# Two decode layers on one core: attention by groups of four heads from one row of DRAM, with more kept on chip for the second layer

## The chip, the cores and the metric

The kernel runs on one core of a Trainium2 chip. The metric is device time in microseconds, taken over three runs of the kernel. The profile is one execution recorded by the hardware profiler.

## What is computed

Four sequences (B = 4), one token each, 640 features, float32. Attention and a gated MLP are applied twice, in turn, with the same weights and the same caches:

```python
x = A_x
x = x + _A_ref(_layernorm(x), A_k_cache, A_v_cache, A_wq, A_wo)
x = x + _B_ref(_layernorm(x), B_W_gate, B_W_up, B_W_down)
x = x + _A_ref(_layernorm(x), A_k_cache, A_v_cache, A_wq, A_wo)
x = x + _B_ref(_layernorm(x), B_W_gate, B_W_up, B_W_down)

# _A_ref: 32 heads of 128, the last W = 1024 of 4096 cached keys
q = (x @ wq).reshape(B, 1, 32, 128).transpose(0, 2, 1, 3)
p = softmax(einsum("bhqd,bhkd->bhqk", q, k) * 128 ** -0.5)
o = einsum("bhqk,bhkd->bhqd", p, v)
return o.transpose(0, 2, 1, 3).reshape(B, 1, 4096) @ wo

# _B_ref: F = 1728
gate, up = x @ W_gate, x @ W_up
return (gate * (gate > 0) * up) @ W_down
```

Per layer the four caches and matrices are 329,024 floats for each of the 128 partitions. All the arithmetic is one row per sequence, so each weight and each cached key is used once or four times and then not needed until the second layer.

## The kernel before

Everything that is read more than once lies in one SBUF tile, `store`, of 54,560 floats per partition. `heads` in DRAM holds for each of the 32 heads one block of 128 rows of 9,472 floats: 640 of the query weights (WQ), 4,096 of keys (KK), 4,096 of values (VV), 640 of the output weights (WO). `mlp` holds the MLP's 25,920 floats per partition: the gate and up weights in four parts (the last part, narrower, first), then the down weights.

**Loads.** `todo` (lines 67 to 107) is the list of loads in order, written out by hand. `load` (115) issues the next one on SP's DMA queue into the ring `store` as soon as its whole place is free; `done` (144) marks a place free after the last product that reads it and calls `load` again. SP issues in order, so a load that waits for its place holds all later ones back. The program order of the products thus sets which product each load waits for. Loads of the first 27 heads are whole heads. Heads 27 (its second half) to 31 stay on chip for layer two: in layer one they go to the front of `store`, up to FRONT = 42,624, and `done` does not free them. The first MLP uses what lies behind FRONT, 11,936 floats. Layer two takes the heads in the order 27 to 31, 0 to 26 (line 66).

**Attention** (313) works head by head, one ahead: the query of the next head (230: five products of 128 columns, with the normalized x repeated eight times to fill 32 rows), its scaling on VectorE (240) and turn (244), then for a head the scores (250: eight products of 512 columns, one for each sequence and half of the keys, four of them side by side in the four column strips of TensorE), softmax on VectorE and ScalarE (262), the turn of the probabilities (269: eight transposes), the values (278: eight products of 512 columns), the sums (290), the turn of the four sequences' outputs (296) and the projection into `y` (305). `y` stays in PSUM and gathers the residual.

**The MLP** (352) works in four parts: gate and up products (358), ReLU and product (369), a turn (378), the down products (391).

Between the stages `normalized` (182) and `deviation` (212) do the layer norm from `y`; `go_on` (224) puts the residual back into `y`. The last two lines of the kernel copy `y` and store it.

Of the kernel before, what the change touches and what calls it, by code (L numbers as in the profile page):

```python
# [21 lines left out]
WQ, KK, VV, WO = 0, D, D + 4096, D + 8192  # L22
HALF = D + 4096
HEAD = 2 * HALF

# [8 lines left out]

STORE = 54560
KEPT = 5

FRONT = KEPT * HEAD - HALF  # L40
FIRST, FIRST_MLP = 10928, 51880


CUTS = {
    "head": [*range(WQ, KK, P), *range(KK, WO, 512), *range(WO, HEAD + 1, QUARTER)],
    "mlp": [*range(0, GU0, P), *range(GU0, WD0, 256), WD0, TAIL, *range(WD1, MLP + 1, D)],
}
# [3 lines left out]
def decode_kernel(ctx: ExitStack, tc: tile.TileContext, x, heads, mlp, sel, out):  # L51
# [4 lines left out]
    ps_s = ctx.enter_context(tc.tile_pool(name="ps_s", bufs=1, space=bass.MemoryType.PSUM))  # L56
    ps_p = ctx.enter_context(tc.tile_pool(name="ps_p", bufs=2, space=bass.MemoryType.PSUM))
    ps_o = ctx.enter_context(tc.tile_pool(name="ps_o", bufs=1, space=bass.MemoryType.PSUM))
    ps_y = ctx.enter_context(tc.tile_pool(name="ps_y", bufs=1, space=bass.MemoryType.PSUM))
    ps_m = ctx.enter_context(tc.tile_pool(name="ps_m", bufs=2, space=bass.MemoryType.PSUM))  # L60
# [5 lines left out]
    order = [list(range(H)), list(range(H - KEPT, H)) + list(range(H - KEPT))]  # L66
    todo = []

    def pieces(layer, kind, i, *cuts):
        for lo, hi in zip(cuts, cuts[1:]):  # L70
            todo.append((layer, kind, i, lo, hi))

    def half_a(layer, h, step=4096):
        pieces(layer, "head", h, WQ, *range(KK + step, VV, step), VV)

    def half_b(layer, h, step=4096):
        pieces(layer, "head", h, VV, *range(VV + step, WO, step), HEAD)

    for h in range(H - KEPT):
        pieces(0, "head", h, 0, HEAD)  # L80
    split = H - KEPT
    half_b(0, split)
    half_a(0, split)
    half_a(0, split + 1)
    for h in range(split + 1, H - 1):
        half_a(0, h + 1)
        pieces(0, "head", h, VV, WO)

    pieces(0, "head", H - 1, VV, VV + 3072, WO)
    for h in range(split + 1, H):  # L90
        pieces(0, "head", h, WO, HEAD)
    pieces(0, "mlp", 0, 0, *[c for j in range(3) for c in (GU0 + j * GU, GU0 + j * GU + 2048)],
           WD0, WD1 + WD, WD1 + 2 * WD, MLP - 2 * D, MLP - D, MLP)
    half_b(1, split, 2048)
    steps = [2048] * 6 + [4096] * 2
    half_a(1, 0, steps[0])
    for h in range(7):
        half_a(1, h + 1, steps[h + 1])
        half_b(1, h, steps[h])
    half_b(1, 7)  # L100
    for h in range(8, split):
        pieces(1, "head", h, 0, HEAD)
    pieces(1, "mlp", 0, 0, *range(GU0 + GU, WD0 + 1, GU), *range(WD1 + WD, MLP - WD + 1, WD),
           MLP - 2 * D, MLP - D, MLP)

    jumps = {(0, "head", split, 0): 0, (0, "mlp", 0, 0): FIRST_MLP, (1, "head", split, VV): FRONT}
# [3 lines left out]
    at = FIRST  # L110
    source = {"head": heads, "mlp": mlp}

    held = {}

    def load(part=False):

        nonlocal at
        while todo:
            layer, kind, i, lo, end = todo[-1]
            at = jumps.pop((layer, kind, i, lo), at)  # L120
            hi = max(c for c in CUTS[kind] + [end] if c <= min(end, lo + STORE - at))
            if hi <= lo:
                at = FRONT if layer == 0 and kind != "head" else 0
                continue
            if any(live[at:at + hi - lo]):
                n = live.index(True, at) - at
                hi = max([lo] + [c for c in CUTS[kind] if c <= lo + n])
                if not part or hi < lo + 512:
                    return
            todo.pop()  # L130
            if hi < end:
                todo.append((layer, kind, i, hi, end))
            live[at:at + hi - lo] = [True] * (hi - lo)
            held.setdefault((layer, kind, i), []).append((lo, hi - lo, at))
            nc.sync.dma_start(out=store[:, at:at + hi - lo], in_=source[kind][i][:, lo:hi])
            at += hi - lo

    def get(key, lo, n):
        for first, m, p in held[key]:
            if first <= lo and lo + n <= first + m:  # L140
                return store[:, p + lo - first:p + lo - first + n]
        raise KeyError((key, lo, n))

    def done(key, lo, n):

        if key[1] == "head" and key[0] == 0 and (key[2] > split or key[2] == split and lo < VV):
            return
        for first, m, p in held[key]:
# [9 lines left out]
    sel_sb = const.tile([P, P + 40], F32, name="sel_sb")  # L158
# [3 lines left out]
    nc.vector.memset(eps_sb, EPS)  # L162

# [323 lines left out]
```

## Time and profile before

| | |
|---|---|
| three runs | 755.49, 757.39 (median), 758.18 us |
| profiled execution, span from first to last instruction | 754.4 us |
| runs' median less that span | 2.95 us |
| read from DRAM | 315.19 MB |
| loads issued on SP's queue | 101 of heads, 22 of the MLP |
| busy TensorE / weight loads / VectorE / ScalarE | 604.2 / 301.0 / 174.8 / 121.3 us |
| mean granted TensorE clock | 0.832 |

The page gives the profiled execution's span alone; its own time as a run is not among its lines. TensorE's busy time counts overlapping and pipelined products, and the granted clock is a share of full speed. A load's time to landing is counted from its issue, so it includes the time in the queue behind earlier loads.

### The profile page before, as it was taken

What the parts mean: (1) busy time and instruction counts of PE and PEld (TensorE: products, weight loads), DVE (VectorE), ACT (ScalarE), POOL (GpSimd) and SP (SyncE); (2) the same over time, 40 slices, a digit from 0 to 9 for tenths busy, and PEclk for the clock granted to TensorE, in tenths of its full rate; (3) what the DMA queues carried; (4) which work ended last, traced back from release to release, by engine and by line L of the source; (5) the groups of instructions that cost most, each with busy time, mean ns of one, the idle gap of its engine ahead of it and who ended that gap; (6) DMA issues with size and microseconds to landing.
All of it is one profiled execution on the core that took longest, in us unless ns stands there. A gap on an engine that the chain in (4) does not pass through costs nothing.

```text
span 754.4 us, 11650 instructions
## 1 busy us (share of the span) xinstructions
PE 604.2 (80%) x5150; PEld 301.0 (40%) x5150; DVE 174.8 (23%) x495; ACT 121.3 (16%) x218; POOL 0.2 (0%) x4
## 2 busy tenths in 40 slices
PE   0788678787788697888867888888887787797888
PEld 0344343344344243344433444444443343343344
DVE  0222212212212221222211222323221222221221
ACT  1201111111101101112201111111211111111120
POOL 0000000000000000000000000000000000000000
PEclk9988788778878877789997888989988788877878
DMA  9999999999999999999999999999999999999994
GB/s 389 433 423 435 440 421 443 419 437 430 426 437 424 434 427 434 423 427 423 408 378 420 401 414 415 432 434 433 422 428 444 421 441 423 437 423 429 431 423 175
DMA packets 18058, 316.02 MB, mean 419 GB/s; under 512 B 2004, under 2 KB 2644, under 8 KB 4696
## 3 DMA queue, kind: packets, MB, share of 16 engines
q1 hardware_dynamic: 17856, 315.19, 98.2%
q8 instruction: 40, 0.66, 0.3%
q10 hardware_dynamic: 152, 0.10, 0.0%
q14 instruction: 10, 0.08, 0.0%
HBM read 315.19 MB, written 0.08 MB: 418 GB/s over the span
## 4 chain that ended last, share of the span: by engine, by line
DMA 60%; PE 28%; DVE 5%; ACT 4%; issue 3%; SPq 0%; ACTq 0%; DVEq 0%
DMA store<-in_heads 57%; PE ps L257 9%; PE so L300 5%; DVE nm L265 4%; PE pp L275 4%; DMA store<-in_mlp 3%; PE y L309 2%; ACT probs L267 2%; PE gu L365 2%; ACT gates L288 1%; PE so L292 1%; PE qt L246 1%; PE qp L236 1%; PE po L285 1%; PE y L396 1%
## 5 line engine op out<-in xcount | busy, mean ns | idle before, releaser
L257 PE MATMUL ps<-store,qT 128*32 128x512 f32 x1024 | 190.8, 884 | 2.3 <-ACT probs L267 1.3
L267 ACT ACTIVATE probs<-ps,nm 128x1024 f32<-128x1024 f32 x64 | 71.3, 1113 | 558.1 <-DVE nm L265 558.1
L285 PE MATMUL po<-store,pT 128*32 128x512 f32 x1024 | 124.7, 605 | 0.0
L236 PE MATMUL qp<-store,xT 128*32 128x128 f32 x640 | 45.4, 308 | 82.5 <-DMA store<-in_heads 81.4
L300 PE MATMUL so<-sel_sb,gates 128*128 128x1 f32 x512 | 78.9, 275 | 28.2 <-ACT gates L288 28.2
L300 PEld LDWEIGHTS so<-sel_sb,gates 128*128 128x128 f32 x512 | 73.7, 222 | 45.1 <-ACT gates L288 37.9
L236 PEld LDWEIGHTS qp<-store,xT 128*32 128x32 f32 x640 | 28.3, 118 | 133.0 <-DMA store<-in_heads 115.8
L265 DVE TENSOR_REDUCE nm<-ps 128x1 f32<-128x1024 f32 x64 | 77.8, 1215 | 7.5 <-PE ps L257 7.5
L275 PE MATMUL pp<-sel_sb,probs 128*128 128x128 f32 x512 | 77.4, 300 | 0.0
L275 PEld LDWEIGHTS pp<-sel_sb,probs 128*128 128x128 f32 x512 | 72.0, 174 | 0.0
L257 PEld LDWEIGHTS ps<-store,qT 128*32 128x32 f32 x1024 | 38.4, 140 | 75.6 <-issue 63.6
L294 DVE RECIPROCAL r<-so 128x4 f32<-128x4 f32 x64 | 11.7, 183 | 224.6 <-PE so L292 224.6
L292 PEld LDWEIGHTS so<-sel_sb,sm 128*128 128x128 f32 x128 | 24.9, 243 | 89.8 <-issue 84.3
L242 DVE TENSOR_SCALAR qs<-qp,rstd 128x128 f32<-128x128 f32 x64 | 22.4, 351 | 146.1 <-PE qp L236 145.9
L285 PEld LDWEIGHTS po<-store,pT 128*32 128x32 f32 x1024 | 26.9, 109 | 50.2 <-DVE pT L276 29.4
L276 DVE COPY pT<-pp 128x128 f32<-128x128 f32 x128 | 37.3, 292 | 38.1 <-PE pp L275 29.9
L288 ACT COPY gates<-po 128x512 f32<-128x512 f32 x64 | 36.8, 575 | 5.8 <-PE po L285 5.8
L309 PE MATMUL y<-store,oT 128*4 128x160 f32 x512 | 34.8, 354 | 1.6 <-DVE oT L303 0.5
L292 PE MATMUL so<-sel_sb,sm 128*128 128x4 f32 x128 | 30.5, 309 | 1.9 <-ACT probs L267 1.9
L303 DVE TENSOR_TENSOR oT<-so,r 128x4 f32<-128x4 f32 x64 | 10.4, 162 | 89.0 <-PE so L300 89.0
L246 PE MATMUL qt<-sel_sb,qs 128*128 128x4 f32 x128 | 27.5, 285 | 2.9 <-DVE qs L242 2.9
L246 PEld LDWEIGHTS qt<-sel_sb,qs 128*128 128x128 f32 x128 | 24.2, 236 | 4.2 <-DVE qs L242 2.8
(51 smaller groups left out, 123.7 us busy)
## 6 DMA issues: line engine op xcount, KB each, us to landing
store<-in_heads SPq DMA_DIRECT2D x38, 4736.0 KB, 41.7
store<-in_heads SPq DMA_DIRECT2D x10, 2368.0 KB, 40.4
store<-in_heads SPq DMA_DIRECT2D x13, 1344.0 KB, 11.5
store<-in_heads SPq DMA_DIRECT2D x13, 1024.0 KB, 9.7
store<-in_heads SPq DMA_DIRECT2D x2, 3648.0 KB, 37.9
store<-in_heads SPq DMA_DIRECT2D x2, 3392.0 KB, 41.2
store<-in_heads SPq DMA_DIRECT2D x3, 2048.0 KB, 40.2
store<-in_mlp SPq DMA_DIRECT2D x2, 2560.0 KB, 40.5
```

The source lines that it names most:

```text
L236: nc.tensor.matmul(qp[h][32 * g:32 * g + 32, :], xT[:, c], w, start=c < 4, stop=c > 0, tile_position=(0, 32 * g))
L246: nc.tensor.matmul(qt, qs.pop(h), sel_b, start=True, stop=True)
L257: nc.tensor.matmul(ps[32 * b:32 * b + 32, j, :], q[:, b:b + 1].to_broadcast([P, 32]), get(key, lo, 512), start=True, stop=True, tile_posit ...
L265: nc.vector.tensor_reduce(nm, flat, axis=AX.X, op=ALU.max, negate=True)
L267: nc.scalar.activation(probs, flat, AF.Exp, bias=nm, accum_out=sums[h])
L275: nc.tensor.transpose(pp[:, c, :], probs[:, (4 * j + c) * P:(4 * j + c + 1) * P], ident)
L276: nc.vector.tensor_copy(t[:, 4 * j:4 * j + 4], pp[:, :, None, 0:P:32].to_broadcast([P, 4, 8, B]))
L285: nc.tensor.matmul(po[32 * g:32 * g + 32, :], p[:, c], get(key, VV + c * 512, 512), start=c < 4, stop=c >= 4, tile_position=(0, 32 * g))
L288: nc.scalar.copy(gates, po)
L292: nc.tensor.matmul(so[h][:, :B], sums.pop(h).to_broadcast([P, P]), sel_s, start=True, stop=True)
L300: nc.tensor.matmul(s[:, B + b:B + b + 1], gates[:, b * P:(b + 1) * P], sel_b[:, b:b + 1], start=True, stop=True)
L309: nc.tensor.matmul(y[32 * g:32 * g + B], o, get(key, WO + g * QUARTER, QUARTER), start=False, stop=last, tile_position=(0, 32 * g))
```

## The change

Four heads make a group; there are eight groups. `heads` and `mlp` become one array, `stream`, of 128 rows of 329,024 floats: the pieces of all groups and of the MLP in the order in which they are used (q0, k0, q1, v0, o0, k1, q2, ...). A load is a run of columns of it, up to 13,700 floats.

A group is handled as one: its scores go into the same PSUM tile, row 32b + h for sequence b and head h. For that the turned query is written into a cleared tile `qz`, in which the four columns that serve head h are zero but for its own, and the four heads' products are added up in PSUM. One softmax, one turn and one sum then serve four heads. The values products of the four heads lie side by side in the four column strips. The query is one run of five products of 512 columns. A group's projection comes after the first scores of the next group.

Kept for layer two are group 7 (q7, k7, v7, o7), o6 and the last 7,680 floats of v6. They lie in front of KEPT = 48,128; `store` has 55,040 floats, so 6,912 remain behind them, three times SLOT = 2,304, and the first MLP goes through those. Layer two takes the groups in the order 7, 6, 0 to 5.

The shared PSUM tiles `ps`, `po`, `qp`, `ms` replace rotating ones; `go_on` moves behind the first scores, and in the MLP behind the first full gate part.

The core of the diff:

```diff
+GH = 4
+G = H // GH
+WQ, KV, WO = KC * GH * P, GH * 4096, GH * D
...
-STORE = 54560
-KEPT = 5
-FRONT = KEPT * HEAD - HALF
-FIRST, FIRST_MLP = 10928, 51880
+VKEPT = 7680
+SLOT = 2304
+FRONT = VKEPT + WO
+KEPT = FRONT + WQ + 2 * KV + WO
+STORE = KEPT + 3 * SLOT
+FIRST = 0
+LONG = 13700
...
+    steps(0, 0, WQ, 4096, 4096, 8192)
+    run(0, AT["k", 0] + KV, AT["q", 7])
+    run(0, AT["q", 7], AT["q", 7] + WQ, place=FRONT)
+    run(0, AT["v", 6], vsplit)
+    run(0, vsplit, AT["k", 7], place=0)
+    steps(0, AT["k", 7], *[4096] * 7, 2048, 1024, 1024, 1280, 1280, place=FRONT + WQ)
+    todo.append([KEPT])
+    run(0, M0, TOTAL - 3 * D, SLOT)
+    steps(0, TOTAL - 3 * D, 2 * D, D)
+    todo.append([KEPT, FRONT, 0])
+    run(1, AT["q", 6], AT["q", 6] + WQ)
+    steps(1, AT["k", 6], 2048, 2048, 2560, 2048, 2048, 2048, 3584)
+    run(1, AT["q", 0], AT["q", 0] + WQ)
+    run(1, AT["v", 6], vsplit, 4096)
+    run(1, AT["k", 0], AT["q", 6])
+    run(1, AT["v", 5], AT["v", 5] + 12288)
+    steps(1, AT["v", 5] + 12288, 2048, 1024, 1024, 1280, 1280)
+    steps(1, M0, GU0, GU, GU, GU, WD1 - WD0, WD, WD, 1280, 640, 640)
...
+            layer, lo, end, place, most, least = todo[-1]
+            at = state["at"] if place is None else place
+            top = min(end, lo + most, lo + STORE - at)
+            hi = max(c for c in CUTS if c <= top)
...
             if any(live[at:at + hi - lo]):
                 n = live.index(True, at) - at
-                hi = max([lo] + [c for c in CUTS[kind] if c <= lo + n])
-                if not part or hi < lo + 512:
+                hi = max(c for c in CUTS if c <= lo + n)
+                if hi < lo + least:
                     return
...
+            nc.sync.dma_start(out=store[:, at:at + n], in_=stream[:, lo:hi])
...
+    nc.vector.memset(qz, 0.0)
...
+    for t in (y, qp, ps, po):
+        nc.vector.memset(t, 0.0)
...
+            nc.tensor.matmul(qp[q:q + B], xT[:, c], get(layer, lo, GH * P), start=c < 4, stop=c > 0,
+                             tile_position=(0, q))
...
+        nc.vector.tensor_scalar(gates, qp, rstd, SCALE, op0=ALU.mult, op1=ALU.mult)
...
+        for h in range(GH):
+            nc.tensor.matmul(ms[:, h * B:h * B + B], gates[:, h * P:(h + 1) * P], sel_b, start=True, stop=True)
+        nc.vector.tensor_copy(qz[:, turn[0], :, 0:GH * GH:GH + 1],
+                              ms[:, :GH * B].rearrange("p (h b) -> p b h", b=B))
...
-                nc.tensor.matmul(ps[32 * b:32 * b + 32, j, :], q[:, b:b + 1].to_broadcast([P, 32]),
-                                 get(key, lo, 512), start=True, stop=True, tile_position=(0, 32 * b))
+                lo = AT["k", g] + ((h * 2 + j) * B + b) * 512
+                nc.tensor.matmul(ps[32 * b:32 * b + GH, j, :], qz[:, turn[0], b, GH * h:GH * h + GH],
+                                 get(layer, lo, 512), start=h == 0, stop=h == GH - 1, tile_position=(0, 32 * b))
...
+        for c in range(8):
+            for h in range(GH):
+                lo = AT["v", g] + (c * GH + h) * 512
+                nc.tensor.matmul(po[32 * h:32 * h + B], t[:, c, h], get(layer, lo, 512),
+                                 start=c == 0, stop=c == 7, tile_position=(0, 32 * h))
...
+        for g, after in zip(gs, gs[1:] + [None]):
+            scores(layer, g, 0)
+            if before is None:
+                go_on()
+            else:
+                project(layer, before, values_turned(r), False)
+            for h in range(1, GH):
+                scores(layer, g, h)
+            sums = softmax()
+            if after is not None:
+                query(layer, after, xT)
+                query_out(rstd)
+            else:
+                table(AF.Sqrt)
+            r = totals(sums)
+            t = turned()
+            if after is not None:
+                query_turned()
+            values(layer, g, t)
+            before = g
+        project(layer, before, values_turned(r), True)
...
+    attention(0, list(range(G)))
+    forward(0)
+    held[1] += [e for e in held[0] if any(a <= e[0] < b for a, b in kept)]
+    attention(1, [7, 6, *range(6)])
+    forward(1)
```

More of the change, by code (lines that the diff above doesn't have):

```diff
@@ L95, in decode_kernel, with run @@
[L95 to L106, printed above, removed]
+    def run(layer, lo, hi, most=LONG, least=LONG, place=None):
+        todo.append((layer, lo, hi, place, most, least))
@@ L107, in decode_kernel @@
+    steps(1, M0, GU0, GU, GU, GU, WD1 - WD0, WD, WD, 1280, 640, 640)
     todo.reverse()
     live = [False] * STORE
[L110 to L117, printed above, removed]
-        while todo:
[L119 to L123, printed above, removed]
+    state = {"at": FIRST, "bases": [0]}
@@ L240, in query_out @@
[L240 to L253 removed]
+            q = 32 * (c % 4)
@@ L299, in values_turned @@
+    def values_turned(r):
         for b in range(B):
[L300 removed]
+            nc.tensor.matmul(ms[:, b * GH:b * GH + GH], gates[:, b * P:(b + 1) * P], ident[:, b:P:32],
                              start=True, stop=True)
[L302 to L311 removed]
@@ L313, in attention, with project @@
-    def attention(layer):
-        hs = order[layer]
-        load(True)
+        oT = small.tile([P, GH, B], F32, name="oT")
+        nc.vector.tensor_tensor(oT, ms[:, :GH * B].rearrange("p (b h) -> p h b", h=GH),
+                                r.rearrange("p (h b) -> p h b", b=B), op=ALU.mult)
+        return oT
+    def project(layer, g, oT, last):
+        for h in range(GH):
+            for q in range(4):
+                lo = AT["o", g] + h * D
+                nc.tensor.matmul(y[32 * q:32 * q + B], oT[:, h], get(layer, lo + q * QUARTER, QUARTER),
+                                 start=False, stop=last and h == GH - 1, tile_position=(0, 32 * q))
+            done(layer, lo, D)
@@ L316, in attention @@
+    def attention(layer, gs):
+        load()
         xT, d = normalized()
[L317 removed]
+        query(layer, gs[0], xT)
         rstd = deviation(d)
         table(AF.Exp)
[L320 to L339 removed]
```

313 lines of the change are left out of this document (129 added, 184 removed).

## The prediction

> **What bounds the kernel now.** I read the page's head, its queue table and its chain first, to see which resource is full.
>
> ```profile
> span 754.4 us, 11650 instructions
> ...
> q1 hardware_dynamic: 17856, 315.19, 98.2%
> ...
> DMA 60%; PE 28%; DVE 5%; ACT 4%; issue 3%; SPq 0%; ACTq 0%; DVEq 0%
> ```
>
> The load queue keeps the 16 DMA engines busy for 98.2% of the span, and most of the chain is a load. Next comes the table of windows (length, busy time of PE, PEld, DVE, ACT and POOL with counts, granted clock, DMA share, GB/s), to see where the rate is lost.
>
> ```profile
> 20.00:360.00 340.00, 274.82 (x2132) 134.66 (x2133) 79.60 (x217) 53.34 (x95) 0.00 (x0) 0.81 1.00 429
> 360.00:400.00 40.00, 30.23 (x414) 16.20 (x413) 6.61 (x26) 5.72 (x12) 0.00 (x0) 0.91 0.98 394
> 400.00:480.00 80.00, 68.94 (x587) 33.92 (x588) 21.78 (x62) 15.00 (x27) 0.00 (x0) 0.84 1.00 414
> 480.00:700.00 220.00, 182.59 (x1473) 91.16 (x1472) 54.01 (x148) 35.27 (x63) 0.00 (x0) 0.83 1.01 432
> ...
> 700.00:740.00 40.00, 34.03 (x300) 17.56 (x302) 9.71 (x31) 7.97 (x15) 0.00 (x0) 0.79 0.99 421
> 740.00:748.00 8.00, 8.00 (x142) 4.08 (x138) 1.49 (x6) 1.10 (x3) 0.00 (x0) 0.98 0.45 177
> 748.00:754.40 6.40, 3.44 (x93) 2.18 (x82) 0.50 (x2) 0.00 (x0) 0.00 (x0) 0.97 0.04 13
> 2.00:20.00 18.00, 2.14 (x27) 1.22 (x27) 0.87 (x4) 2.86 (x3) 0.00 (x0) 1.00 0.96 411
> ```
>
> Two long stretches run at 429 and 432 GB/s with DMA share 1; I take 430 as the full rate. Against it, in microseconds: 315.19 MB need 733.0; the start costs 2.0 before the first load plus 18 x (1 - 411/430) = 0.8; the middle (first MLP, start of the second layer) 40 x (1 - 394/430) + 80 x (1 - 414/430) = 6.3; the end 0.8 from 700 to 740 and 4.7 from 740 to 748, where the engines finish unevenly; the rest of the span 6.4. The sum is 754.0, so the account closes.
>
> **The change, term by term.** *Bytes.* Kept for layer two before: 4.5 heads of 9,472 floats, 42,624 per partition. After: group 7 (37,888), the last 7,680 of v6 and o6 (2,560): 48,128. So 5,504 floats x 512 B = 2.82 MB less is read, 312.37 MB, 726.4 us at 430: 6.6 saved. The mix of pieces matters too, since small ones run slower (windows again, then two groups of DMA issues with KB each and us to landing):
>
> ```profile
> 410.00:440.00 30.00, 25.14 (x219) 12.38 (x223) 8.89 (x24) 6.24 (x11) 0.00 (x0) 0.89 0.99 401
> ```
>
> ```profile
> store<-in_heads SPq DMA_DIRECT2D x13, 1344.0 KB, 11.5
> store<-in_heads SPq DMA_DIRECT2D x13, 1024.0 KB, 9.7
> ```
>
> Those 26 pieces make 410 to 440 run at 401, a loss of 2.0 us. The new load list comes to 95 loads instead of 123: pieces of 6.8 MB in the long stretches, about 1 to 2 MB in the first layer's last group, in its MLP and for the first dozen loads of the second layer.
>
> *PE, DVE and ACT.* A group does once what each head did: 16 reductions, exponentials, totals and value copies instead of 64, and 128 transposes instead of 512. The scores and values products stay as many, four rows wide instead of 32. In the long stretches this saves no time, because PE waits for loads there already; that slack is also the cover under which I cost the new joint softmax at nothing.
>
> ```profile
> PEld qp L236 <- DMA store<-in_heads: 115.8, 38, 6.7
> ...
> PE y L172 <- DMA sel_sb<-in_sel: 17.2, 1, 17.2
> ```
>
> The second row covers the four new clearings at the start (qz and three PSUM tiles): DVE does them while PE waits 17.2 us for its first operand. New are also waits on the shared PSUM tile ms: PE may turn the next query only after DVE's reciprocal of the totals, with the group's values products queued behind it. That is some 0.2 us a group (below), on PE, and hidden wherever PE waits for loads.
>
> *First MLP through three slots.* Eleven pieces of about 2,304 floats (2.74 us each at 430) and two small ones go through 6,912 floats, where 11,936 were free before. A slot's next load waits for the products on its piece, and SP, which issues in order, holds every later load behind it. Rows for one round (timeline: start, length, engine, line; then the shortest round trip of a transfer among the DMA issues):
>
> ```profile
> 374.28 0.46 PE L309 MATMUL y<-store,oT 128*4 128x160 f32 x8 [0.25 <-DVE oT L303]
> ...
> 376.79 1.18 PE L365 MATMUL gu<-store,xT 128*32 128x128 f32 x27 [0.44 <-DVE d L208]
> ...
> 378.51 2.37 PE L365 MATMUL gu<-store,xT 128*32 128x256 f32 x40
> ```
>
> ```profile
> out_x<-probs SPq DMA_DIRECT2D x1, 80.0 KB, 1.6
> ```
>
> Twenty products take 2.37 us, so a slot's nine take 1.07. A small store lands 1.6 us after its issue, which I take as the delay of a refill. 1.07 + 1.6 = 2.7 us must fit under the 5.5 us of two other slots: it does. At the entry, three pieces land during 8.1 us after the last of o7; two heads of projection (0.9), 2.1 us from there to the first gate product, 1.7 to the second gate, two products (0.2) and 1.6 make 6.5: it just fits. So 0 to 9 us (the top is worked out below), and I take 1.
>
> *Start of the second layer.* Group 7 is on chip, and its products free the room for everything else. From the last MLP piece, loads of 51,200 floats can follow (q6, k6, v6, k0, part of v0), 61.0 us at 430; the next wait for group 6's projection. PE must by then have done the rows below.
>
> ```profile
> 400.25 0.46 PE L396 MATMUL y<-store,hT 128*4 128x160 f32 x8 [0.94 <-DMA store<-in_mlp]
> ...
> 405.84 3.61 PE L257 MATMUL ps<-store,qT 128*32 128x512 f32 x16 [0.25 <-DVE qT L248]
> ...
> 421.52 0.46 PE L309 MATMUL y<-store,oT 128*4 128x160 f32 x8
> 421.79 1.90 PE L257 MATMUL ps<-store,qT 128*32 128x512 f32 x16
> 423.62 0.39 PE L292 MATMUL so<-sel_sb,sm 128*128 128x4 f32 x2
> 423.87 1.07 PE L275 MATMUL pp<-sel_sb,probs 128*128 128x128 f32 x8
> 424.05 0.18 DVE L294 RECIPROCAL r<-so 128x4 f32<-128x4 f32 x1 [2.35 <-PE so L292]
> 424.89 1.92 PE L285 MATMUL po<-store,pT 128*32 128x512 f32 x16
> 425.18 1.21 DVE L265 TENSOR_REDUCE nm<-ps 128x1 f32<-128x1024 f32 x1
> 426.51 1.11 ACT L267 ACTIVATE probs<-ps,nm 128x1024 f32<-128x1024 f32 x1 [6.35 <-DVE nm L265]
> 428.25 1.05 PE L300 MATMUL so<-sel_sb,gates 128*128 128x1 f32 x8 [1.02 <-ACT gates L288]
> ```
>
> Last MLP product to first scores: 5.6 us, plus 1.8 for a query four times as wide, 7.4. Group 7: scores 4 x 1.72 (start to start in such a run) = 6.9, softmax 2.6, totals, transposes and query turn 2.5, values 6.9: 18.9. Then one head of scores, the values' turn (1.05 + 0.4) and four projections (1.84): 5.0; the rest of group 6 17.2; the same 5.0 again: 53.5 at full clock, of which about 44 scale with PE's clock. At the granted 0.83 it is 62.5; with 1.6 for the issue, 3.1 us more than the loads cover. So 0 to 3; I take 3. **Middle in all: 4**, against 6.3.
>
> *Start and end.* The start stays 2.8: the first load is issued as before. For the engines' uneven finish I keep 5 of 5.5. What follows the last landing shrinks, since PE was behind:
>
> ```profile
> 749.08 2.36 PE L396 MATMUL y<-store,hT 128*4 128x160 f32 x64
> 749.19 0.17 DVE L383 COPY hT<-ph 128x16 f32<-128x16 f32 x1 [1.71 <-PE ph L382]
> 751.51 0.32 DVE L428 COPY probs<-y 128x160 f32<-128x160 f32 x1 [2.14 <-PE y L396]
> ```
>
> Only 0.46 of products stay behind the last 320 KB piece, with 0.3 for the semaphore and 2.9 from the copy at 751.51 to the span's end: 3.7 instead of 6.4. PE can be ready: the last V piece is 512 KB, and the 13.3 MB of MLP weights behind it give it 30.9 us.
>
> **Sum**: 726.4 + 2.8 + 4 + 5 + 3.7 = 741.9 us of span. The median of the runs, 757.39, stands 3.0 over the profiled span, so I predict **744.8**.
>
> **Rivals.** *A. The second layer's PE chain is late.* At clock 0.75 the 44 us become 58.4, the idle time 8.7, and the time 751. For: every later load hangs on the projections. Against: 0.83 is already an average with softmax waits in it.
>
> *B. The three slots starve the DMA.* Before, the first MLP did run dry with more room:
>
> ```profile
> 376.00:386.00 10.00, 8.11 (x155) 5.04 (x154) 2.18 (x10) 1.30 (x4) 0.00 (x0) 1.00 0.89 333
> ```
>
> At 333 its 13.3 MB take 39.9 us instead of 30.9: +9, 754. The Trainium skill, DMA: Bandwidth & Descriptors, section "Bandwidth", measured 341 GB/s for copies of 1 MB; by that the MLP would take an estimated 38.9 us. The trace speaks against it: its 1,024 and 1,344 KB pieces, queued, ran at 401.
>
> *C, slower. Four-row products do not hold the clock.* If scores and values run at 0.5, the 44 us become 87.6 and the DMA idles 37.9: 780. It decides from clock 0.65, where the idle time reaches 18 us. Against: the 64 four-row products at 749.08 ran while 0.97 was granted; but they last 2.4 us, not 14.
>
> *D, slower. One row of DRAM.* Each partition's run now lies 1,316,096 B from the next, where heads lay 37,888 B apart. If that costs rate, every load pays: at 401 the bytes take 779, and the time is 797; it decides below 421. The trace has only narrower pitches; the MLP rows, 103,680 B apart, carry most of 700 to 740 at 421. The Trainium skill, DMA: Bandwidth & Descriptors, section "Latency and other measured facts", found copies between DRAM tensors slowed at row pitches of large powers of two, and cured by 4 KiB of padding. 1,316,096 is five times 256 KiB plus 5,376, so by that rule the loss should be small; no run here shows it.
>
> **Chances.** The forecast (738 to 749) 0.68; A 0.10, B 0.06; C 0.07, D 0.05; within 0.3% (A and B together) 0.04. A measurement of this kernel tells about 0.3% from no change. That makes faster 0.84, same 0.04, slower 0.12. Low end: no idle middle and 2 us less at the end, 738.5. High end: past A and B, 755; C, D and no change lie outside it.
>
> **What would show it.** Right: about 312.4 MB read, 95 loads, 430 GB/s in the long stretches, 3 to 5 us of DMA idle around the first MLP and the second layer's start, the span ending some 4 us behind the last landing. Bytes and tail are the surest terms. Wrong: long stretches under 425 (D), a granted clock under 0.7 at the second layer's start with SP waiting for its projections (A, C), SP waiting for gate products with DMA share under 0.9 (B).

## The result, and the profile after

| | before | after |
|---|---|---|
| median of 7 runs each | 756.42 us (754.2 to 758.18) | 751.13 us (749.08 to 753.39) |
| ratio | | 0.9927, 95% interval 0.9907 to 0.9946 |
| profiled execution: run, span | span 754.4 us | run 752.2, span 750.4 us |
| mean granted clock of that execution | 0.832 | 0.787 |

The change saves 5.3 us; 12.6 were forecast from the 757.39 then known, with 738 to 749 as the likely range. The new kernel is faster, by less than half of what was forecast. The head of its profile and its load queue:

```profile
span 750.4 us, 8175 instructions
...
PE 488.3 (65%) x3806; PEld 158.3 (21%) x3806; DVE 59.0 (8%) x163; ACT 42.2 (6%) x74; POOL 0.2 (0%) x4
...
q1 hardware_dynamic: 13824, 312.37, 97.9%
```

The bytes fell as reckoned, 315.19 to 312.37 MB, and VectorE and ScalarE now do a third of what they did (174.8 and 121.3 us before). The queue is as full as it was. To find what was lost, the windows of the new kernel (length, busy time of PE, PEld, DVE, ACT and POOL with counts, granted clock, DMA share, GB/s):

```profile
2.00:20.00 18.00, 6.83 (x53) 2.97 (x53) 3.40 (x10) 4.61 (x6) 0.00 (x0) 1.00 1.00 421
20.00:360.00 340.00, 215.23 (x1496) 65.45 (x1496) 22.73 (x54) 15.22 (x25) 0.00 (x0) 0.78 1.00 431
360.00:380.00 20.00, 14.53 (x151) 6.36 (x151) 1.75 (x9) 1.45 (x4) 0.00 (x0) 0.65 0.80 313
380.00:400.00 20.00, 13.13 (x151) 4.95 (x155) 1.58 (x7) 1.10 (x3) 0.00 (x0) 0.83 0.95 362
400.00:420.00 20.00, 14.72 (x127) 5.88 (x116) 2.28 (x10) 2.04 (x4) 0.00 (x0) 0.59 0.83 312
420.00:440.00 20.00, 19.05 (x165) 6.40 (x164) 2.87 (x6) 1.79 (x3) 0.00 (x0) 0.98 1.01 412
440.00:460.00 20.00, 18.78 (x174) 6.13 (x173) 3.04 (x7) 1.20 (x2) 0.00 (x0) 0.91 1.04 442
360.00:480.00 120.00, 94.34 (x893) 35.91 (x897) 14.45 (x45) 9.37 (x19) 0.00 (x0) 0.82 0.94 378
480.00:700.00 220.00, 138.86 (x952) 40.16 (x944) 11.98 (x31) 7.74 (x13) 0.00 (x0) 0.76 1.00 432
700.00:736.00 36.00, 22.91 (x262) 9.84 (x262) 4.59 (x17) 4.87 (x10) 0.00 (x0) 0.79 0.99 415
740.00:744.00 4.00, 3.90 (x70) 1.49 (x66) 0.61 (x3) 0.37 (x1) 0.00 (x0) 0.80 0.89 357
744.00:750.40 6.40, 2.74 (x64) 1.19 (x56) 0.32 (x1) 0.00 (x0) 0.00 (x0) 0.85 0.18 65
```

The long stretches run at 431 and 432 GB/s. The loss sits in 60 us: the first MLP and the step into the second layer, 313, 362 and 312 GB/s with DMA shares of 0.80, 0.95 and 0.83. Against 430 GB/s, 360 to 480 loses 120 x (1 - 378/430) = 14.5 us. The same window of before:

```profile
360.00:480.00 120.00, 99.17 (x1001) 50.12 (x1001) 28.39 (x88) 20.72 (x39) 0.00 (x0) 0.86 1.00 407
```

There it was 6.4 us. The account of after closes: bytes 726.4, start 2.0 + 18 x (1 - 421/430) = 2.4, middle 14.5, end 36 x (1 - 415/430) + 4 x (1 - 357/430) + 6.4 x (1 - 65/430) = 7.4, in all 750.7 for a span of 750.4.

What happens where the rate falls first shows the timeline at the entry to the first MLP (start, length, engine, line, operation; in brackets the idle time before it and what ended it):

```profile
362.81 1.03 PE L299 MATMUL po<-store,pT 128*4 128x512 f32 x4 [0.25 <-DMA store<-in_stream]
...
365.90 2.13 PE L317 MATMUL y<-store,oT 128*4 128x160 f32 x32 [0.27 <-DVE oT L309]
...
370.16 2.09 PE L364 MATMUL ps<-store,xT 128*4 128x128 f32 x27 [0.25 <-DVE d L221]
...
373.45 0.28 DVE L374 SCALAR_TENSOR_TENSOR gates<-ps,rstd,gates 96x64 f32<-96x64 f32 x1 [0.38 <-ACT gates L373]
...
373.79 4.44 PE L364 MATMUL ps<-store,xT 128*4 128x256 f32 x38 [1.26 <-DVE gates L374]
...
374.88 3.73 SPq L146 DMA_DIRECT2D store<-in_stream  x3
...
380.15 1.01 PE L364 MATMUL ps<-store,xT 128*4 128x256 f32 x2 [1.93 <-DMA store<-in_stream]
```

The last values product needs PE until 363.84; only at 374.88 does SP issue the next load (line 146), the first into a slot that the gate products have freed. By the list of loads it takes the first slot, which holds the first gate part and the first 256 columns of the second, so it waits for two products of the second part. Between these two times the three pieces in the slots land, 8.1 us at 430, and then nothing is in flight; two windows show it:

```profile
366.00:370.00 4.00, 3.46 (x51) 2.04 (x44) 0.74 (x4) 0.29 (x1) 0.00 (x0) 0.52 1.01 423
370.00:376.00 6.00, 4.58 (x62) 2.49 (x66) 0.83 (x5) 0.57 (x2) 0.00 (x0) 0.50 0.35 121
```

From 370 to 376 the DMA engines are busy 0.35 of the time. PE in turn waits 1.93 us for that load at 380.15: the pause has come back to it.

### The profile page after: what moved, and what is told of

It reads as the page before. It is cut to its first block, busy times and chain, and to the rows that moved or that the text cites. A ratio compares the mean times of both kernels' runs of the same rounds, so it can differ in the third digit from the quotient of the medians.

```text
span 750.4 us, 8175 instructions
## 1 busy us (share of the span) xinstructions
PE 488.3 (65%) x3806; PEld 158.3 (21%) x3806; DVE 59.0 (8%) x163; ACT 42.2 (6%) x74; POOL 0.2 (0%) x4
## 3 DMA queue, kind: packets, MB, share of 16 engines
q1 hardware_dynamic: 13824, 312.37, 97.9%
HBM read 312.37 MB, written 0.08 MB: 416 GB/s over the span
## 4 chain that ended last, share of the span: by engine, by line
DMA 74%; PE 21%; another core or an unknown queue 2%; DVE 1%; ACT 1%; issue 1%; SPq 0%; ACTq 0%; DVEq 0%
DMA store<-in_stream 74%; PE ps L266 6%; PE po L299 5%; PE y L317 2%; PE ps L364 2%; PE ms L306 2%; PE qp L246 1%; PE ms L257 1%; PE pp L290 1%; PE y L394 0%; SPq L146 0%; PE y L237 0%; DVE oT L309 0%; PE ms L279 0%
## 5 line engine op out<-in xcount | busy, mean ns | idle before, releaser
L266 PE MATMUL ps<-store,qz 128*4 128x512 f32 x1024 | 170.3, 720 | 97.4 <-DMA store<-in_stream 96.7
L299 PE MATMUL po<-store,pT 128*4 128x512 f32 x1024 | 163.9, 747 | 75.5 <-DMA store<-in_stream 75.5
L266 PEld LDWEIGHTS ps<-store,qz 128*4 128x4 f32 x1024 | 30.7, 96 | 207.1 <-issue 112.4
L246 PE MATMUL qp<-store,xT 128*4 128x512 f32 x160 | 41.4, 761 | 28.8 <-DMA store<-in_stream 28.3
L275 ACT ACTIVATE probs<-ps,nm 128x1024 f32<-128x1024 f32 x16 | 17.8, 1113 | 311.9 <-DVE nm L273 311.9
L273 DVE TENSOR_REDUCE nm<-ps 128x1 f32<-128x1024 f32 x16 | 19.6, 1225 | 194.9 <-PE ps L266 194.9
L306 PEld LDWEIGHTS ms<-sel_sb,gates 128*128 128x128 f32 x128 | 19.6, 234 | 20.5 <-issue 17.1
L306 PE MATMUL ms<-sel_sb,gates 128*128 128x4 f32 x128 | 21.0, 287 | 1.5 <-ACT gates L302 1.5
L290 PE MATMUL pp<-sel_sb,probs 128*128 128x128 f32 x128 | 20.4, 312 | 0.0
L257 PE MATMUL ms<-sel_sb,gates 128*128 128x4 f32 x128 | 17.7, 261 | 2.9 <-DVE gates L251 2.9
L257 PEld LDWEIGHTS ms<-sel_sb,gates 128*128 128x128 f32 x128 | 17.8, 214 | 3.2 <-DVE gates L251 3.1
L290 PEld LDWEIGHTS pp<-sel_sb,probs 128*128 128x128 f32 x128 | 18.3, 175 | 0.0
L364 PEld LDWEIGHTS ps<-store,xT 128*4 128x4 f32 x300 | 9.7, 108 | 28.9 <-issue 12.6
## 6 DMA issues: line engine op xcount, KB each, us to landing
store<-in_stream SPq DMA_DIRECT2D x11, 2048.0 KB, 29.6
```

What stands on the lines that cost most here:

```text
L246: nc.tensor.matmul(qp[q:q + B], xT[:, c], get(layer, lo, GH * P), start=c < 4, stop=c > 0, tile_position=(0, q))
L257: nc.tensor.matmul(ms[:, h * B:h * B + B], gates[:, h * P:(h + 1) * P], sel_b, start=True, stop=True)
L266: nc.tensor.matmul(ps[32 * b:32 * b + GH, j, :], qz[:, turn[0], b, GH * h:GH * h + GH], get(layer, lo, 512), start=h == 0, stop=h == GH - ...
L273: nc.vector.tensor_reduce(nm, flat, axis=AX.X, op=ALU.max, negate=True)
L275: nc.scalar.activation(probs, flat, AF.Exp, bias=nm, accum_out=sums)
L290: nc.tensor.transpose(pp[:, c, :], probs[:, (4 * j + c) * P:(4 * j + c + 1) * P], ident)
```

## The experiments

Three theories. **Room**: with three slots behind the kept part, fewer bytes are in flight than the DMA moves in the time from a landing to the refill, at the entry and again at the step into the second layer. **Clock**: TensorE's granted clock, 0.50 from 366.1 to 386.6 in the trace of after, makes the products that free the slots late. **Shared tile**: the second gate part waits until VectorE has read the first from the same PSUM tile `ps` (the 1.26 us at 373.79). The two parts use different halves of that tile. Every edit is against the kernel after.

**Two tiles for the gate parts.** They go in turn to `ps` and `qp`, so that the second part needn't wait for VectorE.

```diff
+        gus = ps[:, 0], qp
...
-                    nc.tensor.matmul(ps[32 * g:32 * g + B, j % 2, :2 * n], xT[:, c], get(layer, lo, 2 * n),
+                    nc.tensor.matmul(gus[j % 2][32 * g:32 * g + B, :2 * n], xT[:, c], get(layer, lo, 2 * n),
...
-            gu = ps[:, j % 2]
+            gu = gus[j % 2]
```

> Gate parts alternate between the first half of ps and the tile qp, which the MLP does not use, so that a gate part no longer waits for VectorE to read the part before (1.26 + 0.53 + 0.65 us at 373 to 388 in the changed kernel). If that shared tile is what makes the DMA run dry (theory 3), the first refill starts 1.3 us earlier, the DMA share of 360 to 380 rises from 0.80 to about 0.87, and the time falls by 2 to 4 us. If the room of three slots (theory 1) or the clock (theory 2) decides, the wait is gone but the time falls by at most 1.3 us.

Measured: 750.23 us (747.01 to 751.73), 0.9909 [0.9875, 0.9943] of before. In its timeline the second gate part starts as the first ends, with no wait, and the refill is issued 3.3 us after the first gate product, where it was 4.7 (370.16 to 374.88):

```profile
369.70 2.10 PE L365 MATMUL qp<-store,xT 128*4 128x128 f32 x27 [0.25 <-DVE d L221]
...
371.92 4.15 PE L365 MATMUL ps<-store,xT 128*4 128x256 f32 x37
...
373.00 9.84 SPq L146 DMA_DIRECT2D store<-in_stream  x4
```

Its windows at the entry, through the down products, and at the step into the second layer:

```profile
366.00:376.00 10.00, 9.02 (x128) 4.78 (x127) 1.74 (x9) 0.86 (x3) 0.00 (x0) 0.66 0.77 296
386.00:403.00 17.00, 9.54 (x135) 3.25 (x138) 1.12 (x5) 0.54 (x2) 0.00 (x0) 0.87 0.89 326
403.00:421.00 18.00, 15.60 (x111) 5.71 (x107) 2.23 (x9) 2.04 (x4) 0.00 (x0) 0.55 0.88 339
```

The first of them was 242 in after, so the wait did cost the entry something; but 326 and 339 (361 and 311 in after) say that the later pauses stay. The whole gains 0.9 us, less than the runs spread.

**More room and longer pieces.** 5,120 floats fewer are kept, so that 12,032 lie behind the kept part, and the MLP's pieces grow to 4,010.

```diff
-VKEPT = 7680
-SLOT = 2304
+VKEPT = 2560
+SLOT = 4010
...
-STORE = KEPT + 3 * SLOT
+STORE = 55040
```

> 2,560 instead of 7,680 floats of v6 are kept, so the first MLP has about 12,030 floats in three slots of 4,010, the room of the kernel before. 2.62 MB more are read: +6.1 us at 430 GB/s. Theory 1 (the room is too small for the time from landing to refill): the stretch 360 to 420 goes from 329 GB/s back to about 400, which gives back 9 to 10 us, so the time falls by 3 to 4 us in all. Theory 2 (TensorE's half clock between 366 and 386 and between 403 and 421 makes the chains long, whatever the room): half of the loss stays, and the time rises by 1 to 3 us.

Measured: 750.26 us (749.48 to 750.69), 0.9914 [0.9889, 0.9939]. It reads 314.99 MB, 2.62 more than after, 6.1 us at 430. Two windows, of the first pause and of the MLP's second half:

```profile
370.00:376.00 6.00, 3.97 (x54) 2.25 (x58) 0.44 (x2) 0.57 (x2) 0.00 (x0) 0.50 1.00 423
386.00:403.00 17.00, 13.59 (x194) 5.41 (x194) 2.26 (x11) 1.27 (x4) 0.00 (x0) 0.84 0.78 308
```

The pause at the entry is gone (423 for 121), at the same granted clock of 0.50. A new one stands at the MLP's end. The 6.1 us of bytes were earned back, and no more.

**Gate products of 32 rows.** The normalized x stands eight times side by side, as before the change, so that the products fill 32 rows.

```diff
+            nc.vector.tensor_tensor(xT, pt[:, :, None, :B].to_broadcast([P, KC, 8, B]),
+                                    mu[:, None, None, :].to_broadcast([P, KC, 8, B]), op=ALU.subtract)
...
-                    nc.tensor.matmul(ps[32 * g:32 * g + B, j % 2, :2 * n], xT[:, c], get(layer, lo, 2 * n),
+                    nc.tensor.matmul(ps[32 * g:32 * g + 32, j % 2, :2 * n], xT[:, c], get(layer, lo, 2 * n),
```

> The gate and up products of both MLPs take the normalized x eight times, 32 rows wide, as the kernel before did; all else as changed. If four-row gate products are too thin to release the clock (theory 2a), the granted clock of 370 to 386 rises from 0.50 to 0.8 or more, the gate parts take 2.4 instead of 4.1 us, and the time falls by 2 to 5 us. If the clock follows only how long TensorE waits, it stays at 0.5 there and the time within 1 us.

Measured: 750.65 us (745.84 to 751.75), 0.9906 [0.9867, 0.9945]. The clock was hardly raised at the entry (0.56 from 366 to 376, where after has 0.51), and the pause stayed (250 GB/s for 242). The profiled run was granted 0.91 at the step into the second layer and ran at 403 there, where after has 0.53 and 311:

```profile
403.00:421.00 18.00, 15.44 (x145) 4.83 (x133) 3.44 (x10) 2.04 (x4) 0.00 (x0) 0.91 0.99 403
```

That profile suggests that the clock has a part there; it doesn't show it. The runs spread over 6 us, and the median moves by 0.5.

**Filler products.** PE gets more work ahead of the entry: five rounds of four products into `qp` among the values of layer one's last group. Their results aren't read.

```diff
+    def filler(t):
+        for h in range(GH):
+            nc.tensor.matmul(qp[32 * h:32 * h + B], t[:, 0, h], probs[:, :512], start=True, stop=True,
+                             tile_position=(0, 32 * h))
...
+            if layer == 0 and g == G - 1 and c >= 4:
+                filler(t)
...
+        if layer == 0 and g == G - 1:
+            filler(t)
```

> Five rounds of filler products (four side by side, 512 columns, 0.86 us each at full clock) into the idle tile qp while TensorE waits for the last pieces of v7 in the first layer; nothing reads them. Theory 2b (waiting for the small pieces of v7 lowers the clock at 366): the clock stays 1.0 from 357 to at least 376, the entry into the first MLP is 1.5 to 2 us shorter, and the time falls by 1.5 to 3 us. Otherwise the clock still falls at 366 to 370 and the time stays within 1 us or rises by the last filler round, 0.3 us.

Measured: 751.51 us (749.75 to 752.71), 0.9919 [0.9886, 0.9952]. Two windows at the entry, then the last group's projection and the refill:

```profile
366.00:370.00 4.00, 3.73 (x48) 1.74 (x43) 0.17 (x1) 0.59 (x1) 0.00 (x0) 1.00 1.02 429
370.00:376.00 6.00, 4.18 (x81) 2.74 (x71) 1.35 (x8) 0.86 (x3) 0.00 (x0) 0.72 0.26 107
...
369.49 1.27 PE L326 MATMUL y<-store,oT 128*4 128x160 f32 x32 [0.27 <-DVE oT L318]
...
377.37 3.16 SPq L146 DMA_DIRECT2D store<-in_stream  x3
```

From 366 to 370 the clock was 1.00, for 0.52 in after, and the DMA stopped all the same, with a share of 0.26 where after has 0.35. But this doesn't clear the clock. The filler's own products stood ahead of the entry, so the projection began at 369.49 instead of 365.90; from there to the refill it took 7.9 us, for 9.0 in after. And the clock was back at 0.50 from 372.6 to 379.4, when the gate products ran.

**Pieces of half a slot.** The same room, but by the list of loads seven pieces, of 512 to 1,152 floats, lie in it at the entry instead of three.

```diff
-    run(0, M0, TOTAL - 3 * D, SLOT)
+    run(0, M0, TOTAL - 3 * D, SLOT // 2)
```

> The first MLP goes through the same 6,912 floats in pieces of up to 1,152 floats instead of 2,304: seven in flight instead of three, the first freed in the middle of the first gate part. If the refill's grain decides (theory 1a: a refill hangs on the landing and the products of a whole piece), the entry gap of 4.3 us at 366 to 376 falls under 2, 360 to 403 goes from 335 to about 385 GB/s and the time falls by 3 to 5 us. If only the number of floats in the room decides (theory 1b), the gaps stay and the time is within 1 us, or up to 1 us longer by the smaller packets.

Measured: 748.15 us (745.78 to 749.87), 0.9881 [0.984, 0.9921]: 3.0 better than after, at the edge of what the spread lets one tell. The entry goes from 242 to 310, the step into the second layer stays at 309 (311):

```profile
366.00:376.00 10.00, 7.90 (x121) 4.36 (x125) 1.57 (x8) 0.86 (x3) 0.00 (x0) 0.66 0.86 310
403.00:421.00 18.00, 16.02 (x110) 5.42 (x114) 1.72 (x8) 1.75 (x3) 0.00 (x0) 0.62 0.85 309
```

A smaller piece is freed sooner, which shortens the way from landing to refill; the bytes in flight are the same.

**More room, same pieces.** 12,032 floats of room, pieces of 2,304.

```diff
-VKEPT = 7680
+VKEPT = 2560
...
-STORE = KEPT + 3 * SLOT
+STORE = 55040
```

> 2,560 floats of v6 kept as in the run with more room, but pieces of 2,304 as in the changed kernel, so five in flight. 2.62 MB more: +6.1 us. Theory 1 in either form: the DMA share of 360 to 420 comes to 0.98 or more and the rate to 410, which gives back 11 us, so the time falls by 4 to 6 us. If the gaps are the clock's, the gain is under 2 us.

Measured: 749.04 us (748.55 to 749.65), 0.9895 [0.986, 0.993], with 6.1 us more of bytes. As with the longer pieces, the entry is whole (421) and a pause stands before 403:

```profile
386.00:403.00 17.00, 12.90 (x177) 4.90 (x174) 1.81 (x9) 0.66 (x2) 0.00 (x0) 0.81 0.78 305
```

The reason is in the list of loads: after the MLP the ring starts again at KEPT, where with this room the last MLP pieces happen to lie. The second layer's first loads, q6 and k6, wait for the last down products, while the rest of the room is empty.

**Half pieces with two tiles; the same with wide gate products.** Edits from above put together: half pieces and the two gate tiles, then the 32 rows as well.

```diff
-    run(0, M0, TOTAL - 3 * D, SLOT)
+    run(0, M0, TOTAL - 3 * D, SLOT // 2)
...
+        gus = ps[:, 0], qp
```

> Half pieces and the two gate tiles together. The wait on VectorE's reading of the gate part before stands between the first gate parts, so it should cost only where a refill hangs on it: 1 to 2 us less than half pieces alone if it does, the same if the small pieces already cover it.

> As the run before, with gate products 32 rows wide. Theory 2a: the clock stays at 1.0 more often between 377 and 411, so the query and first scores of the second layer run at full speed, and the gap of 2 us near 417 goes: 1 to 2 us less than the run before. If the clock follows the waits alone, the same within 1 us.

Measured: 749.27 us (747.99 to 751.53), 0.989 [0.9842, 0.9937], and 748.62 us (747.16 to 750.41), 0.989 [0.9851, 0.993]. Neither beats half pieces alone. With half pieces, the shared tile and the wide products have nothing further to give that the runs can tell. At the entry, from 366 to 376, the first was granted 0.66 and the second 0.83 of the clock, and they ran at 341 and 336 GB/s.

**More room, ring restarted elsewhere.** The same room of 12,032, and the second layer's first loads start 2,560 floats further on.

```diff
-    todo.append([KEPT, FRONT, 0])
+    todo.append([KEPT + 2560, FRONT, 0])
```

> As the run with the same pieces and more room (2,560 floats of v6 kept), but the second layer's first loads go on in the ring behind the last MLP pieces instead of starting again at KEPT, where those pieces lie; so they wait for gate and first down products and not all for the very last one. Theory 1: that restart is what left the DMA idle for 4.0 us at 386 to 403 there; the stretch 360 to 420 rises from 388 to 415 GB/s and the time falls by 4 us more, to about 745. If the pause there is the chain of products itself (theory 2), it stays within 1 us.

Measured: 746.51 us (745.9 to 748.36), 0.9866 [0.9839, 0.9893]. The stretch that stood at 305 runs at 417, and the next one, which had run at 425, falls to 355:

```profile
386.00:403.00 17.00, 12.88 (x173) 4.74 (x174) 1.84 (x9) 0.66 (x2) 0.00 (x0) 0.80 1.02 417
403.00:421.00 18.00, 15.32 (x94) 5.09 (x93) 3.34 (x6) 2.95 (x5) 0.00 (x0) 0.73 0.92 355
```

That shows where the former kernel's pause came from. Moving the start removed it, but q6 and the first of k6 are now loaded sooner, and the loads behind them still wait for group 7's query and first scores.

**Four slots.** 2,560 floats fewer are kept than after: room for 9,472, four pieces of 2,304 in flight.

```diff
-VKEPT = 7680
+VKEPT = 5120
...
-STORE = KEPT + 3 * SLOT
+STORE = 55040
```

> 5,120 floats of v6 kept, room 9,472, pieces of 2,304: four in flight, and the ring happens to end so that q6 waits for the first down products. 1.31 MB more than the changed kernel, +3.05 us. Theory 1: idle time at the entry under 1 us, 2 to 3 us left at the second layer's start; the time 3 to 5 us under the changed kernel's. Theory 2: within 1 us of it or longer.

Measured: **743.14 us** (742.88 to 743.41), 0.9816 [0.979, 0.9841]. The stretch of the first pause, and the step into the second layer:

```profile
370.00:376.00 6.00, 4.74 (x61) 2.30 (x58) 0.44 (x2) 0.57 (x2) 0.00 (x0) 0.50 0.92 346
403.00:421.00 18.00, 15.57 (x110) 5.77 (x114) 3.97 (x9) 2.79 (x5) 0.00 (x0) 0.86 1.01 422
```

It reads 1.31 MB more than after (313.68 MB), 3.05 us, and is 8.0 us faster, more than the 3 to 5 expected. From 360 to 480 it runs at 423, which loses 120 x (1 - 423/430) = 2.0 us. The ring ends elsewhere with this room, too: q6 waits for the down products of the first full part, where in after it waits for those of the second. It beats both kernels, and its interval doesn't meet that of after.

**Four slots, half pieces.** The four slots with pieces of 1,152 floats.

```diff
-VKEPT = 7680
+VKEPT = 5120
...
-STORE = KEPT + 3 * SLOT
+STORE = 55040
...
-    run(0, M0, TOTAL - 3 * D, SLOT)
+    run(0, M0, TOTAL - 3 * D, SLOT // 2)
```

> The same room in pieces of up to 1,152. If the grain matters once there is room, 1 to 2 us less than the run before; if the room alone does, the same within 1 us.

Measured: 746.25 us (743.86 to 746.64), 0.985 [0.9816, 0.9883]: 3.1 slower than with whole pieces, the other way than with three slots. The step into the second layer fell from 422 to 346:

```profile
403.00:421.00 18.00, 15.94 (x102) 4.84 (x94) 2.61 (x5) 2.38 (x4) 0.00 (x0) 0.71 0.90 346
```

Why the half pieces harm there wasn't settled. By the lists of loads q6 and the first of k6 wait for the same products in both kernels. The clock in that window was 0.71, that of the four slots 0.86; whether it is the reason or follows from later loads, no run shows.

**Two slots.** What is kept stays as in after; a third of the room is taken away.

```diff
-STORE = KEPT + 3 * SLOT
+STORE = KEPT + 2 * SLOT
```

> The changed kernel with 2,304 floats less behind KEPT: two slots, the same bytes. Theory 1: each refill now has one piece of cover, 2.7 us, against a round trip of about 4 us, and the entry loses a further 2.7 us: 360 to 403 falls to 250 GB/s or less and the time rises by 12 to 20 us. Theory 2: the loss is that of the long chains at the entry and at the second layer's start, so the time rises by about 3 us.

Measured: 771.05 us (766.74 to 773.81), 1.0165 [1.012, 1.021]: slower than before, with the bytes of after, and 19.9 us above after, as the room theory expected.

```profile
370.00:376.00 6.00, 4.71 (x56) 2.09 (x49) 0.44 (x2) 0.57 (x2) 0.00 (x0) 0.50 0.17 37
380.00:400.00 20.00, 13.28 (x101) 4.21 (x89) 0.94 (x4) 0.73 (x2) 0.00 (x0) 0.66 0.71 261
```

**All of them in one account.** From each profile, which is one execution: the bytes at 430, the loss in the window from 360 to 480 against 430, and what is left of the span.

| kernel | span | bytes | GB/s, 360 to 480 | loss | left |
|---|---|---|---|---|---|
| two slots | 771.9 | 726.4 | 324 | 29.6 | 15.9 |
| after (three) | 750.4 | 726.4 | 378 | 14.5 | 9.5 |
| three, two tiles | 748.6 | 726.4 | 381 | 13.7 | 8.5 |
| three, filler | 749.7 | 726.4 | 383 | 13.1 | 10.2 |
| three, wide gates | 746.7 | 726.4 | 392 | 10.6 | 9.7 |
| three, half pieces | 746.9 | 726.4 | 392 | 10.6 | 9.9 |
| three, half pieces, two tiles | 748.4 | 726.4 | 385 | 12.6 | 9.4 |
| the same, wide gates | 745.2 | 726.4 | 395 | 9.8 | 9.0 |
| four, half pieces | 744.9 | 729.5 | 411 | 5.3 | 10.1 |
| four slots | 741.2 | 729.5 | 423 | 2.0 | 9.7 |
| 12,032, longer pieces | 748.5 | 732.5 | 410 | 5.6 | 10.4 |
| 12,032, same pieces | 747.2 | 732.5 | 412 | 5.0 | 9.7 |
| 12,032, ring moved | 746.4 | 732.5 | 417 | 3.6 | 10.3 |

Apart from two slots, whose long stretch also ran slower (422 GB/s from 480 to 700, 4.1 us; why wasn't tried), what is left is 8.5 to 10.4 us everywhere. So the differences in time are bytes plus the loss in the middle, and from two to four slots that loss falls with the room: 29.6, 14.5, 2.0.

At the entry the room is shown to be the cause. From 370 to 376 the granted clock was 0.50 with two, three and four slots and with the longer pieces in 12,032 floats, and the rate was 37, 121, 346 and 423 GB/s; with the same pieces in 12,032 floats it was 417 at 0.51. The shared tile is worth 1.4 us of the refill there and doesn't close the pause.

At the step into the second layer, from 403 to 421, the rate rises with the room too (235, 311 and 422 GB/s with two, three and four slots), but so does the granted clock (0.50, 0.53 and 0.86). The seven kernels with three slots ran there at 309 to 339 where the clock was 0.53 to 0.65, and at 347 to 403 where it was 0.80 to 0.91. A late load also makes PE wait, so the low clock can have lengthened the pause or followed from it; how much of the room's effect goes through the clock stays open.

More room than four slots saved nothing here: with 12,032 floats 3.6 to 5.6 us of the middle are still lost, and the bytes take 3.0 us more than with four slots.

## Why the prediction was right and wrong

**Right: bytes, rate, start and end.** 312.37 MB and 95 loads were read, the long stretches ran at 431 and 432. The start lost 2.4 us (2.8 forecast), the end 7.4 (5 and 3.7). PE was ready at the end, as the timeline shows: 0.45 us of products behind the last piece, then the copy, 2.9 us ahead of the span's end:

```profile
746.99 0.45 PE L394 MATMUL y<-store,hT 128*4 128x160 f32 x8 [0.33 <-DMA store<-in_stream]
747.51 0.32 DVE L426 COPY probs<-y 128x160 f32<-128x160 f32 x1 [3.57 <-PE y L394]
```

**Mis-sized: the 3.0 over the span.** The run that was profiled stands 1.8 over its span (752.2 and 750.4). The other 1.2 was chance: a median of three runs was set against the span of one execution, and seven runs of before have a median of 756.42, 1.0 under that of the three.

**Wrong: "Middle in all: 4".** It was 14.5, and it is more than the whole miss of 6.3: 10.5 us over, against 1.7 under at start and end and 2.2 in the median over the span (751.13 and 750.4 stand 0.7 apart, where 3.0 was added; the profiled run was slower than the median). The last 0.3 is what the account exceeds the span by.

*The step at the entry, "make 6.5: it just fits".* From the last values product at 363.84 to the issue of the refill at 374.88 it took 11.0 us, against 8.1 us of pieces. The parts, from the timeline above: copy, turn and scaling of the group's outputs 2.1, left out, since the forecast let them run ahead of the last of o7; the projection of all four heads 2.1 where two heads at 0.9 were counted; from there to the first gate product 2.1, as forecast; first to second gate product 3.6, for 1.7, of which 1.26 is the wait for VectorE behind the shared tile, which the forecast didn't see; the products up to the issue 1.1, for 0.2. The delay of the issue, 1.6 in the forecast, comes on top. At the granted 0.50, 38 gate product records took 4.44 us where 40 took 2.37 before. A term that had "just" fitted with rows taken at full clock needed that allowance.

*The refill round, "2.7 us must fit under the 5.5 us of two other slots: it does".* With three slots the MLP's middle ran at a share of 0.95, so the step nearly held; but the two-slot kernel, whose cover is the other slot's 2.74, ran at 261 GB/s with a share of 0.71 inside the MLP, from 380 to 400. The round is longer than the 2.7 of the sum. One part of it was mis-sized: from the refill's issue at 374.88 to the product that waited for it, 380.15, it took 5.3 us, of which the piece itself needs 2.74 at 430, so that the delay is some 2.5 us where the landing of a small store had given 1.6.

*The start of the second layer.* The forecast checked the far end of that chain: 51,200 floats of loads against the products up to group 6's projection. The DMA stopped at the near end. By the list of loads the slots take q6 and 4,096 floats of k6, 7.9 us at 430; the next 2,560 floats go where q7 lay and wait for group 7's query, and all further ones wait for its scores. PE's products, two of SP's waits between 403 and 425 (us in total, times, longest), and the window of the second pause:

```profile
404.61 1.78 PE L394 MATMUL y<-store,hT 128*4 128x160 f32 x24 [0.30 <-DMA store<-in_stream]
...
408.48 2.72 PE L246 MATMUL qp<-store,xT 128*4 128x512 f32 x9 [0.25 <-DVE d L221]
...
415.72 3.60 PE L266 MATMUL ps<-store,qz 128*4 128x512 f32 x16 [0.28 <-DVE qz L258]
...
SPq L146 <- PE ps L266: 10.2, 5, 5.2
...
SPq L146 <- PE qp L246: 5.4, 1, 5.4
...
417.00:420.00 3.00, 3.00 (x14) 0.65 (x6) 0.00 (x0) 0.00 (x0) 0.00 (x0) 0.50 0.47 107
```

q6 was issued only at 403.58, when a down product gave its place back; that is the first pause, with a DMA share of 0.58 from 403 to 406. The last load into the slots went out at 406.45, the one into q7's place at 412.08, and the next at 417.67, after the first half of a head of scores. From the last MLP product (406.39) to the first scores it took 9.3 us, for 7.4. The step that failed is that only the sum of loads was set against the sum of products, not each load against the product that frees its place. With four slots the window from 403 to 421 ran at 422, where after has 311.

**The rivals.** B, the three slots starving the DMA, had the mechanism at the entry, and its sign came (SP waiting for gate products, a DMA share of 0.80 from 360 to 380); 0.06 was too small a chance, and its 754 was 3 us too dear. The Trainium skill, DMA: Bandwidth & Descriptors, section "Bandwidth", gives 341 GB/s for copies of 1 MB (issued there from GpSimd). Here it isn't the piece that sets the rate, since with four slots pieces of about that size run at 411 over the 27 us from 376 to 403. A's 751 is the time that was measured, by luck: SP's waits at the second layer's start were for down products, a query and scores, not for the projections that A named, and from 420 to 460 the DMA ran at 412 and 442, with PE busy for 37.8 of 40 us. C came only at the edge: the first scores ran at 0.50, until 420.8, but from there to 460, mostly four-row scores and values, 0.98 and 0.91 were granted. D didn't come: the long stretches, where it would have shown, ran at 431 and 432. That agrees with the Trainium skill's rule on row pitches of large powers of two (DMA: Bandwidth & Descriptors, "Latency and other measured facts"), 1,316,096 B not being one. The 401 that D and B used was laid to 26 small pieces, wrongly: they are 31.5 MB, 73 us at 430, and can't all lie in the 30 us from 410 to 440. A slower outcome was there to be had: with two slots it is 771.05.

With the middle at 2.0, as four slots give it, the sum of the prediction is 729.5 + 2.8 + 2.0 + 5 + 3.7 = 743.0 of span, where 741.2 was profiled.

## What to carry to other kernels

Space kept for reuse is paid for out of the space that keeps loads in flight: the last 2,560 floats kept here saved 3.05 us of bytes and cost 12.5 us in the middle (14.5 - 2.0, in the profiled executions). Reckon the room from the longest time between a landing and the issue that refills its place, layer norms, stage changes and a halved clock included, and at each change of stage separately; the steady round inside a stage is the mildest case. A chain that "just fits" with durations at full clock should be costed as a miss.

## What the runs showed of the hardware

TensorE's granted clock stood at half for long while PE had work. Windows of after:

```profile
376.30:379.80 3.50, 1.93 (x18) 0.43 (x10) 0.00 (x0) 0.00 (x0) 0.00 (x0) 0.50 0.93 342
383.20:386.60 3.40, 3.40 (x36) 1.17 (x32) 0.00 (x0) 0.00 (x0) 0.00 (x0) 0.50 0.87 298
...
386.00:390.00 4.00, 2.42 (x29) 0.71 (x21) 0.53 (x2) 0.37 (x1) 0.00 (x0) 0.92 0.93 341
```

It stayed at 0.50 from 366.1 to 386.6 and again from 403.7 to 420.8, and then four-row products of 512 columns held 0.98. These four changes lie 20.5, 17.1 and 17.1 us apart, which is 6, 5 and 5 times 3.41 us. Both times the clock came back at the end of such a step in which PE was busy throughout (3.40 of 3.40 us above, and the same from 417.3 to 420.7). The gate products of 4.44 us from 373.79 on filled no step: in the one from 376.3 PE was busy for 1.93 us and then waited for its load. How much of a step must be busy wasn't tried.

Around the pauses the DMA engines are busy without moving the full rate. In the last row above they are busy 0.93 of the time and move 341 GB/s, 367 for a full share, where the long stretches move 431. From 360 to 420 the shares of 0.80, 0.95 and 0.83 account for 20 x (0.20 + 0.05 + 0.17) = 8.4 us of idle time, the rates for 20 x (3 - (313 + 362 + 312)/430) = 14.1. The other 5.7 us are packets that took longer. It isn't only the start after a pause: with half pieces in three slots the engines were busy without a break from 386 to 403 (share 1.03) and moved 389. What makes the packets longer there wasn't separated.
